# Loading and transposing q and k by units of 192 tokens at the start of a fused attention and feed-forward kernel

## Chip, cores and metric

The kernel runs on one core of a Trainium2 chip. The metric is device time in microseconds (us). The kernel before takes 339.88 us, the median of three runs (338.89 to 340.19). A run over 1.5% above the fastest of its kernel would count as slow. A kernel that ran only once is marked below.

## What is computed

```python
# q, k, v: (8 batches, 8 heads, 576 tokens, 64), fp32
scores = q @ k.T / sqrt(64)                 # per batch and head
mask   = (0 <= i - j) & (i - j < 64)        # sliding window of 64 tokens, causal
attn   = softmax(where(mask, scores, -1e9)) @ v
x      = attn as (4608 tokens, 512)
out    = (relu(x @ w_gate) * (x @ w_val)) @ w_out     # 512 -> 1536 -> 512
```

## The kernel before

A **unit** is 192 tokens of all 8 heads; a batch of 576 tokens is three units. A **tile** of the feed-forward part is two units (384 tokens), so twelve tiles follow each other on TensorE (PE), and the attention of later units is woven between their matmuls. Each instruction stands in its engine's queue in the order in which the program issues it (after the change, GpSimd's trace has the next weights at 24.95 us, behind the cast that the program puts before them and that starts at 24.49). The parts that matter here:

```python
U, UB, G = 192, 3, 4          # tokens of a unit, units of a batch, heads of one half
# S = 576, D = 64; row p = (h, i) of 128 holds 18 tokens of one head: token = 18 i + j

def qk_load(b, name, hh):                       # fp32 -> fp16 cast in GpSimd's DMA
    tile_ = nat[b, name, hh] = a_in.tile([128, S // 32 * D], FP16, ...)
    src = (q if name == "q" else k)[b, G * hh:G * hh + G]
    nc.gpsimd.dma_start(tile_, src.rearrange("h (i j) d -> (h i) (j d)", i=32))

def k_first(hh):                                # k of batch 0: fp32, SyncE's hardware queue
    k32 = nat["k32", hh] = x_sb.tile([128, S // 32 * D], FP32, ...)
    nc.sync.dma_start(k32, k[0, G * hh:G * hh + G].rearrange("h (i j) d -> (h i) (j d)", i=32))
# k_round: ScalarE casts k32 to fp16.  qk_trans: VectorE transposes 128x576 into kT or qT.
# ... cut ...
def w_load(wt, src, f0, f1, landed):            # 512 KB (fp16) of weights, GpSimd's DMA
    ...
    nc.gpsimd.dma_start(dst, part)

# start of the program (cut)
for hh in range(2): k_first(hh)
for hh in range(2): qk_load(0, "q", hh)
heat(12, ...)                                   # dummy matmuls
bands(); constants(); v_ones(1, nc.vector)      # masks on GpSimd, fixed values on VectorE
# then, by planned time: transposes of k and q, v_load(0), v_load(1), the six pieces of
# gate and value weights, v_load(2), three pieces of output weights, q and k of batch 1, ...
```

`v_low` copies 64 rows of the values, so that the 128 rows of a matmul hold the 64 tokens before a window as well. `st` is a score matmul, `pv` the product with the values, `sT` the transposed row sums, `xt` the normalised result that the hidden layer `h` reads, `op` the output matmul.

The softmax here doesn't subtract the row's maximum and nothing guards it: scores larger than these inputs give would overflow.

Of the kernel before, what the change touches and what calls it, by code (L numbers as in the profile page):

```python
# [12 lines left out]
MUL = mybir.AluOpType.mult  # L13

# [28 lines left out]
def kernel(  # L43
# [10 lines left out]
    nc = tc.nc  # L54
# [32 lines left out]
    v16s = [persist.tile([128, UB, H, 128], FP16, name=f"v16_{i}") for i in range(UB)]  # L87
# [27 lines left out]
    def v_ones(i, eng):  # L115
        eng.memset(v16s[i][64 if i == 0 else 0:, 0, :, 64:128], 1.0)
        for w in range(1, UB):
            eng.memset(v16s[i][:, w, :, 64:128], 1.0)  # L118

    def k_zeros():  # L120
        nc.vector.memset(kTs[1][:, :, 0:64], 0.0)

    def constants():
        nc.vector.memset(kTs[0][:, :, 0:64], 0.0)
        nc.vector.memset(v16s[0][0:64, 0], 0.0)
        nc.vector.memset(ones, 1.0)
        nc.vector.memset(ones0, 1.0)
        nc.vector.memset(ones0[0:64], 0.0)

# [40 lines left out]
    def k_first(hh):  # L170

        k32 = nat["k32", hh] = x_sb.tile([128, S // 32 * D], FP32, name="k32", bufs=2)
        nc.sync.dma_start(k32, k[0, G * hh:G * hh + G].rearrange("h (i j) d -> (h i) (j d)", i=32))

    def k_round(hh, part, parts):
        n = S // 32 * D // parts
        if part == 0:
            nat[0, "k", hh] = a_in.tile([128, S // 32 * D], FP16, name=f"k{hh}", bufs=2)
        nc.scalar.copy(nat[0, "k", hh][:, n * part:n * part + n], nat["k32", hh][:, n * part:n * part + n])  # L179
# [8 lines left out]
    def v_load(u):  # L188
        b, uu = divmod(u, UB)
        for w in range(UB):  # L190
            k0 = U * uu + 64 * w
            nc.gpsimd.dma_start(v16s[uu][64:128, w, :, 0:64], v[b, :, k0:k0 + 64].rearrange("h p d -> p h d"))  # L192

    def v_low(u):

        uu = u % UB
        if uu > 0:
            nc.vector.tensor_copy(v16s[uu][0:64, 0, :, 0:64], v16s[uu - 1][64:128, UB - 1, :, 0:64])
        nc.vector.tensor_copy(v16s[uu][0:64, 1:UB, :, 0:64], v16s[uu][64:128, 0:UB - 1, :, 0:64])
# [72 lines left out]
    def u_pv(u, cs=(0, 2, 1, 3)):  # L272
# [3 lines left out]
        v16 = v16s[u % UB]  # L276
# [25 lines left out]
    def u_pv_wide(u):  # L302

        d = units[u]
        v16 = v16s[u % UB].rearrange("p w h d -> p w (h d)")
# [60 lines left out]
    def plan_unit(u, T, exp=0.8, mask=1.5, pv=3.9, copy=(4.7, 6.0), norm=(4.8, 6.1, 7.4, 8.7), gap=0.6):  # L366
# [3 lines left out]
        W.at(T + (3.3 if u == 2 else 1.4 if u < 6 else -2.0), lambda: v_low(u))  # L370
# [14 lines left out]
    def ready(n):  # L385
        while normed[0] < n:
            W.pop()
# [96 lines left out]
    with tc.manual_schedule():  # L484
        for hh in range(2):
            k_first(hh)
        for hh in range(2):
            qk_load(0, "q", hh)
# [6 lines left out]
        heat(12, units[0]["st"][1][3])  # L495
        bands()
        constants()
        v_ones(1, nc.vector)
        for hh in range(2):
            for part in range(2):  # L500
                k_round(hh, part, 2)
        W.at(5.0, lambda: qk_trans(0, "k", 0, 0, 9))
        W.at(5.1, band_bias)
        W.at(5.2, lambda: qk_trans(0, "k", 0, 9, 18))
        W.at(7.0, lambda: qk_trans(0, "q", 0))
        W.at(8.6, lambda: qk_trans(0, "k", 1, 0, 9))
        W.at(8.7, lambda: qk_trans(0, "k", 1, 9, 18))
        W.at(9.9, lambda: qk_trans(0, "q", 1))
        G3, V3, O3 = ([(wt, src, f0, f0 + 4) for f0 in (0, 4, 8)]
                      for wt, src in ((wg, moe_w_gate), (wv, moe_w_val), (wo, moe_w_out)))  # L510
        W.at(5.5, lambda: v_load(0))
        W.at(5.6, lambda: v_load(1))
        W.at(6.4, lambda: w_load(*G3[0], 13.7))
        W.at(6.5, lambda: w_load(*V3[0], 16.3))
        W.at(6.6, lambda: w_load(*G3[1], 18.9))
        W.at(9.9, lambda: w_load(*V3[1], 21.5))
        W.at(9.9, lambda: w_load(*G3[2], 24.1))
        W.at(9.9, lambda: w_load(*V3[2], 26.7))
        W.at(12.3, lambda: v_load(2))
        W.at(12.6, lambda: w_load(*O3[0], 31.2))  # L520
        W.at(12.7, lambda: w_load(*O3[1], 33.8))
        W.at(12.8, lambda: w_load(*O3[2], 36.4))
        plan_batch(1, None, (37.0, 37.8, 39.4, 40.8))
        W.at(13.0, lambda: qk_load(1, "k", 0))
        W.at(13.0, lambda: qk_load(1, "k", 1))
        W.at(13.0, lambda: qk_load(1, "q", 0))
        W.at(13.0, lambda: qk_load(1, "q", 1))
        W.at(13.1, lambda: v_load(3))
        W.at(30.0, lambda: v_load(4))
        W.at(30.1, lambda: v_load(5))  # L530
        W.at(5.3, lambda: u_bias(0))
        W.at(5.4, lambda: heat(11, units[0]["spare"], False))
        W.at(8.7, lambda: u_st(0, (0,)))
        W.at(9.5, lambda: heat(11, units[0]["spare"], False))
        W.at(11.0, lambda: u_st(0, (1,)))
        for g in range(G):
            W.at(9.6 + 0.05 * g, lambda g=g: u_exp(0, g, 0))
            W.at(11.1 + 0.05 * g, lambda g=g: u_exp(0, g, 1))
            W.at(12.0 + 0.05 * g, lambda g=g: u_copy(0, g))
            W.at(12.3 + 0.05 * g, lambda g=g: u_exp(1, g))  # L540
        W.at(11.4, lambda: u_pv(0, (0, 1)))
        W.at(11.35, lambda: u_bias(1, (2, 3)))
        W.at(11.5, lambda: u_pv(0, (2, 3)))
        W.at(11.6, lambda: u_bias(1, (0, 1)))
        W.at(11.7, lambda: u_st(1))
        W.at(11.9, lambda: u_sum(0, 0))
        W.at(11.2, lambda: v_low(0))
        W.at(12.15, lambda: v_low(1))
        W.at(12.1, lambda: u_sum(0, 1))
        W.at(12.2, lambda: u_back(0))  # L550
        W.at(12.5, lambda: u_norm(0))
        W.at(12.6, lambda: u_pv(1))
        W.at(12.7, lambda: u_sum(1, 0))
        W.at(12.8, lambda: u_sum(1, 1))
        for n in range(4):
            W.at(12.9, lambda n=n: u_copy(1, n))
        W.at(13.2, lambda: u_back(1))
        W.at(13.3, lambda: u_norm(1))
        W.at(21.0, lambda: v_ones(2, nc.vector))
        W.at(21.0, lambda: v_ones(0, nc.vector))  # L560
        W.at(22.0, k_zeros)
        fast = 0.8, 1.5, 3.9, (4.1, 5.3), (4.2, 5.4, 6.4, 7.5), 0.5
        plan_unit(2, 23.0, 0.8, 1.5, 3.9, (4.7, 6.0), (4.8, 7.4, 11.2, 11.3), 0.6)
        plan_unit(3, 42.15, *fast)
        plan_unit(4, 49.3)
        plan_unit(5, 56.95, *fast)
        T = 67.0
        early, late = (-7.4, -6.0, -4.6, -3.2), (-20.3, -18.9, -17.5, -16.1)
        for t in range(3, NU // 2):
            for u, at, tr in ((2 * t, T + 0.5, early), (2 * t + 1, T + 13.2, late)):  # L570
                if u == 2 * UB:
                    plan_batch(2, 36.9, (49.3, T + 0.3, T + 1.7, T + 3.1))
                elif u % UB == 0:
                    plan_batch(u // UB, at + tr[0] - 10, [at + x for x in tr])
# [3 lines left out]
        W.advance(13.7)  # L578
        ready(1)
        hidden(0, 0, U, 0, 4, 4)  # L580
        ready(2)
# [44 lines left out]
```

## Time and profile before

| | us |
|---|---|
| first score matmul | 8.81 |
| first hidden matmul (tile 0 starts) | 17.00 |
| tile 0 / tile 1 / tile 2 end | 44.06 / 74.77 / 101.86 |
| each later tile | about 25.95 |
| span of the profiled run | 337.9 |

The times in this table and its counterparts are starts and ends of groups of matmuls, read from the trace. From tile 3 on TensorE has no gaps worth naming (busy for 25.95 of 25.95 us in tile 3), so whatever a change is worth must show in the first four rows. The prediction shows the table of busy time by stretch, the chain of waits and TensorE's waits of this kernel. One line also belongs here. It is from the list of DMA issues on the page of the kernel before (destination and source, issuing queue, count, KB each, median us from issue to landing):

```profile
k<-in_k_dram SPq DMA_DIRECT2D x2, 576.0 KB, 4.0
```

Two fp32 loads of 0.59 MB on SyncE's hardware queue landed 4.0 us after their issue (the median of the two), at about 4.4 and 5.8 us. In the microseconds from 3 to 4 and from 4 to 5, 396 and 406 GB/s moved, all of it in packets of SyncE's queue; those of GpSimd's queue start after 5 us.

### The profile page before, as it was taken

The page shows a single profiled execution, that of the slowest core. Times are in us where ns is not written, and L with a number is a line of the kernel's source. Part 1 is how long each engine was busy: PE and PEld are TensorE (multiplying, and loading weights), DVE is VectorE, ACT ScalarE, POOL GpSimd, SP SyncE. Part 2 cuts the span into 40 slices and gives each one's busy share as a digit, 9 for nine tenths or more (in the row PEclk, how much of TensorE's full clock was granted, in tenths as well). Part 3 has the DMA queues.
Part 4 walks back from the last instruction along what each step waited for, and adds up shares of the span by engine and source line. Part 5 has one row for each costly group of instructions (what it writes and reads, how often), then busy time and mean ns, then how long its engine had stood idle before and what let it go on. Part 6 is the DMA issues. An engine that isn't in the chain of part 4 may idle for free.

```text
span 337.9 us, 8605 instructions
## 1 busy us (share of the span) xinstructions
PE 325.5 (96%) x3522; PEld 197.3 (58%) x3522; DVE 260.3 (77%) x493; ACT 176.7 (52%) x383; POOL 74.0 (22%) x121
## 2 busy tenths in 40 slices
PE   8699998999999999999999999999999999999995
PEld 4485485856546656655655655654655664664653
DVE  5878878998998874897989974888889874884430
ACT  4546165745636646645555564564564664653321
POOL 8724341250213221320210410150120200000000
PEclk9989999999999999999999999999999999999999
DMA  8999998496343933491242853296214402001002
GB/s 214 178 206 193 204 203 135 31 139 98 24 77 49 158 51 71 29 185 70 17 53 73 111 75 98 18 143 123 17 10 111 32 3 93 2 2 71 24 0 94
DMA packets 52886, 29.44 MB, mean 87 GB/s; under 512 B 39280, under 2 KB 44272, under 8 KB 52848
## 3 DMA queue, kind: packets, MB, share of 16 engines
q0 software_dynamic: 47088, 18.29, 47.4%
q1 hardware_dynamic: 5616, 10.55, 8.7%
q8 instruction: 27, 0.44, 0.6%
q14 instruction: 11, 0.09, 0.1%
q10 hardware_dynamic: 144, 0.07, 0.1%
HBM read 37.75 MB, written 9.44 MB: 140 GB/s over the span
## 4 chain that ended last, share of the span: by engine, by line
PE 81%; DVE 13%; issue 3%; DMA 2%; ACT 0%; DVEq 0%; ACTq 0%; POOLq 0%
PE h L419 52%; PE op L433 21%; PE pv L311 5%; PE st L249 3%; DVE sT L341 2%; DVE qT L186 2%; DMA q<-in_q_dram 2%; DVE g_sb L407 2%; DVE kT L186 1%; DVE xt L356 1%; DVE rs L350 1%; DVE p L270 1%; PE op L465 1%; DVE v L118 1%; DVE rT L348 0%
## 5 line engine op out<-in xcount | busy, mean ns | idle before, releaser
L419 PE MATMUL h<-xt,wg 128*128 128x384 f16 (+1 forms) x640 | 117.5, 313 | 1.7 <-DVE xt L356 1.7
L419 PE MATMUL h<-xt,wv 128*128 128x384 f16 (+1 forms) x640 | 116.7, 311 | 1.0 <-DVE g_sb L407 1.0
L407 DVE TENSOR_TENSOR g_sb<-r_sb,h 128x384 f16<-128x384 f32 x144 | 78.3, 550 | 48.8 <-PE h L419 47.1
L404 ACT ACTIVATE r_sb<-h 128x384 f32<-128x384 f32 x144 | 70.2, 492 | 67.0 <-PE h L419 55.3
L433 PE MATMUL op<-wo,g_sb 128*128 128x512 f16 x420 | 93.0, 379 | 0.0
L192 POOL DMA_DIRECT2D v<-in_v_dram x72 | 49.5, 696 | 181.0 <-PE pv L311 95.3
L419 PEld LDWEIGHTS <-wg 128*128 128x128 f16 x640 | 61.5, 99 | 36.5 <-DVE xt L356 1.6
L419 PEld LDWEIGHTS <-wv 128*128 128x128 f16 x640 | 59.0, 98 | 31.7 <-issue 1.3
L433 PEld LDWEIGHTS <-g_sb 128*128 128x128 f16 x420 | 40.3, 98 | 46.6
L341 DVE STREAM_TRANSPOSE sT<-pv 64x384 f32<-64x384 f32 x88 | 51.1, 580 | 9.7 <-PE pv L311 7.7
L329 ACT COPY xv<-pv 64x384 f32<-64x384 f32 x88 | 41.6, 473 | 21.5 <-DVE sT L341 8.1
L440 ACT COPY o_sb<-op 128x512 f32<-128x512 f32 x35 | 20.5, 586 | 54.6 <-PE op L433 54.6
L263 ACT ACTIVATE p<-st 128x384 f16<-128x384 f32 x92 | 39.7, 492 | 4.2 <-PE st L249 4.1
L270 DVE TENSOR_TENSOR p<-p,mask 128x384 f16<-128x384 f16 x88 | 27.5, 352 | 0.3 <-ACT p L263 0.2
L350 DVE STREAM_TRANSPOSE rs<-rT 128x768 f32<-128x768 f32 x24 | 23.5, 978 | 0.8
L356 DVE TENSOR_TENSOR xt<-xv,rs 128x768 f16<-128x768 f32 x24 | 22.8, 948 | 0.8
L311 PEld LDWEIGHTS <-v 128*128 128x128 f16 x528 | 18.6, 98 | 4.2 <-issue 0.8
L186 DVE STREAM_TRANSPOSE kT<-k 128x576 f32<-128x576 f32 (+1 forms) x18 | 19.7, 1121 | 1.4 <-ACT k L179 1.3
L311 PE MATMUL pv<-p,v 128*128 128x64 f16 x528 | 19.7, 193 | 1.1 <-DVE p L270 0.6
L186 DVE STREAM_TRANSPOSE qT<-q 128x576 f32<-128x576 f32 x16 | 18.9, 1239 | 1.1 <-DMA q<-in_q_dram 1.1
L249 PEld LDWEIGHTS <-kT 32*128 32x128 f16 x1152 | 11.0, 92 | 10.0 <-issue 9.9
L249 PE MATMUL st<-qT,kT 32*128 32x64 f16 x1152 | 13.9, 189 | 2.3 <-DVE qT L186 2.0
(47 smaller groups left out, 91.8 us busy)
## 6 DMA issues: line engine op xcount, KB each, us to landing
out_dram<-o_sb SPq DMA_DIRECT2D x35, 256.0 KB, 2.0
q<-in_q_dram POOLq DMA_DIRECT2D x16, 288.0 KB, 8.1
v<-in_v_dram POOLq DMA_DIRECT2D x72, 64.0 KB, 3.2
k<-in_k_dram POOLq DMA_DIRECT2D x14, 288.0 KB, 6.1
wg<-in_moe_w_gate_dram POOLq DMA_DIRECT2D x3, 512.0 KB, 10.1
wv<-in_moe_w_val_dram POOLq DMA_DIRECT2D x3, 512.0 KB, 11.9
wo<-in_moe_w_out_dram POOLq DMA_DIRECT2D x3, 512.0 KB, 13.7
k<-in_k_dram SPq DMA_DIRECT2D x2, 576.0 KB, 4.0
```

The source lines that it names most:

```text
L186: nc.vector.transpose(dst.rearrange("p (i j) -> p j i", i=32)[:, j0:j1], src[:, j0:j1])
L192: nc.gpsimd.dma_start(v16s[uu][64:128, w, :, 0:64], v[b, :, k0:k0 + 64].rearrange("h p d -> p h d"))
L249: nc.tensor.matmul(d["st"][hh][g][:, c:c + 64], kT[rows, hh, ks + 64 * w:ks + 64 * w + 128, dh], qT[rows, hh, ks + 64 * w:ks + 64 * w + 64 ...
L263: nc.scalar.activation(d["p"][g].rearrange("p h c -> p (h c)"), d["st"][0][g][:, 0:2 * U], ACT.Exp, scale=scale)
L270: nc.vector.tensor_tensor(p, p, mask[:, None, :].to_broadcast([128, 2 * UB, 64]), MUL)
L311: nc.tensor.matmul(d["pv"][c % 2][:, c // 2, e, 64 * w:64 * w + 64], v16[:, w, 128 * h - 64 * e:128 * h - 64 * e + 128], d["p"][h % G][:, ...
L329: nc.scalar.copy(d["xs"][rows, n::2], d["pv"][n][rows, :, e, 0:U])
L341: nc.vector.transpose(to[64 * e:64 * e + 64, half::2], d["pv"][half][64 - 64 * e:128 - 64 * e, :, e, 0:U])
L404: nc.scalar.activation(part(r_sb), part(h1), ACT.Relu)
L407: nc.vector.tensor_tensor(g_sb[:, f:f + w, c0:c1], part(r_sb), part(h2), MUL)
L419: nc.tensor.matmul(h[:, b * n:b * n + n], wt[:, c, (f + b) * 128:(f + b) * 128 + 128], xt[:, c, c0:c1], start=(c == 0), stop=(c == NC - 1))
L433: nc.tensor.matmul(op, g_sb[:, f, bass.ds(sub * 128, 128)], wo[:, f], start=(f == 0), stop=(f == NF - 1))
```

## The change

The intent: unit 0 needs only its own 192 tokens. So q and k of batches 0 and 1 are loaded, cast and transposed by units; unit 0's loads are spread over the two hardware queues; fewer bytes stand before the weights; the values of a whole batch share one buffer, and the fixed parts of these buffers are set by GpSimd. Its core, with cuts:

```diff
+    J = U // 32
+    def unit_rows(name, u, hh):
+        b, uu = divmod(u, UB)
+        src = (q if name == "q" else k)[b, G * hh:G * hh + G, U * uu:U * uu + U]
+        return src.rearrange("h (i j) d -> h i (j d)", i=32)
+    def unit_load(name, u, hh):                    # units 2 to 5
+        nc.gpsimd.dma_start(unit_tile(name, u, hh), unit_rows(name, u, hh))
+    def unit_load32(name, u, hh, queue):           # units 0 and 1
+        t32 = nat[name, u, hh, 32] = a_in.tile([128, J * D], FP32, ...)
+        queue.dma_start(t32, unit_rows(name, u, hh))
 ...
+        for name in "kq":
+            unit_load32(name, 0, 0, nc.sync)
+            unit_load32(name, 0, 1, nc.scalar)
         for hh in range(2):
-            k_first(hh)
-        for hh in range(2):
-            qk_load(0, "q", hh)
+            for name in "kq":
+                unit_load32(name, 1, hh, nc.sync)
+        v_load(0)
 ...
-        heat(12, units[0]["st"][1][3])
+        heat(7, units[0]["st"][1][3])
 ...
+        for hh in range(2):
+            for name in "kq":
+                unit_round(name, 1, hh, nc.gpsimd.tensor_copy)
+        w_load(*V3[0], 12.8)
+        v_low(1, nc.gpsimd.tensor_copy)
+        heat(6, units[0]["spare"], False)
+        u_pv(0, (0, 1))
 ...
+        for n in (1, 2):
+            w_load(*G3[n], 15.3 + 5.1 * (n - 1))
+            w_load(*V3[n], 17.9 + 5.1 * (n - 1))
+        v_fixed(0, nc.gpsimd, ((UB, NG), (0, UB)))
+        W.at(12.4, lambda: unit_loads(2))
 ...
-        plan_batch(1, None, (37.0, 37.8, 39.4, 40.8))
+        for u, t in ((2, 25.5), (3, 38.0), (4, 45.0), (5, 52.0)):
+            plan_trans(u, t - 2.4)
+            plan_unit(u, t, *(fast if u < 4 else ()))
```

## The prediction

> **What bounds the kernel now.** I read the table of busy time by stretch first, cut where tiles of 384 tokens end on TensorE (its cuts come from the chain of waits). Columns: stretch and length in us, then busy time (instructions) of PE, PEld, DVE, ACT and POOL, granted clock, DMA share, GB/s.
>
> ```profile
> 17.00:44.06 27.06, 26.56 (x236) 17.34 (x236) 22.84 (x43) 11.58 (x26) 9.63 (x15) 0.94 1.40 197
> 44.06:74.77 30.71, 28.24 (x445) 22.74 (x444) 26.60 (x53) 17.99 (x39) 11.45 (x19) 1.00 0.90 125
> 74.77:101.86 27.09, 26.58 (x279) 15.24 (x277) 24.51 (x43) 14.34 (x31) 3.41 (x5) 1.00 0.49 70
> 101.86:127.81 25.95, 25.95 (x278) 15.04 (x277) 20.50 (x41) 14.46 (x31) 6.97 (x11) 1.00 0.60 93
> ```
>
> From tile 3 on TensorE is busy all of each 25.95 us, and the change leaves that steady part alone. What can be won lies before 101.86: 17.00 us before the first hidden-layer matmul, and three tiles that are longer than their matmuls. Their work, from this trace: 48 full-width matmuls take 7.80 us (0.1625 each), 36 output matmuls 7.77, one attention unit 0.48 for its scores and 0.70 for its values. Tile 0, with one unit beside it, needs 15.6 + 7.77 + 1.18 = 24.55; tile 1, with three units and half-width matmuls (16 in 1.32, so 15.84), needs 15.84 + 7.77 + 3.54 = 27.15. So tile 0 loses 2.5, tile 1 3.6 and tile 2 (against 25.95) 1.1 us: **about 7 us after the start, and 17 us of start**.
>
> Then the chain that ended last, within the start (start, length, what):
>
> ```profile
> 1.31 6.16 DMA q<-in_q_dram
> 7.49 1.26 DVE qT L186
> 8.75 1.08 DVE kT L186 x2
> 9.83 1.09 DVE qT L186
> 10.97 0.36 PE st L249 x21
> ...
> 14.91 0.99 DVE rs L350
> 15.99 0.97 DVE xt L356
> ```
>
> The reader should see a transfer, then transposes in a row, then the attention of unit 0. The first scores wait for q of all 576 tokens although unit 0 uses 192. Next the waits of TensorE in tile 1, 44 to 75 us (waiter, what it waited for, total us, times, longest):
>
> ```profile
> PE h L419 <- DVE xt L356: 1.2, 1, 1.2
> PE h L419 <- DVE g_sb L407: 0.7, 1, 0.7
> PE st L249 <- DVE sT L341: 0.3, 1, 0.3
> PE pv L311 <- DVE p L270: 0.3, 1, 0.3
> ```
>
> 2.5 us of tile 1's 3.6: VectorE, 87% busy there, is late. Last, slices of 1 us show what follows a thin start:
>
> ```profile
> 14.00:15.00 1.00, 0.19 (x1) 0.21 (x2) 0.93 (x5) 0.96 (x3) 0.82 (x2) 1.00 1.30 222
> 17.00:18.00 1.00, 0.99 (x7) 0.92 (x7) 1.00 (x4) 0.40 (x2) 0.00 (x0) 0.50 1.25 209
> ```
>
> The granted clock falls to 0.50 from 17 to 20 us: the first 32 hidden matmuls took 4.12 us (17.00 to 21.12) instead of 2.64.
>
> [...]the microsecond from 4 to 5 moved 406 GB/s, and 3 to 4 moved 396. [...]clock 0.50 for about 3 us after four microseconds with 0.69, 0.19, 0.66 and 0.47 us busy. [...]the value copy of 64x1024 takes 0.41 to 0.48 us elsewhere, and 0.65 at 31.01, beside a GpSimd DMA issue. That matters for the casts and memsets that go to GpSimd.
>
> **The change part by part.**
>
> *Loads of unit 0.* Before, k (1.18 MB in fp32), q (1.18) and part of the values stood ahead of the first scores. Now it is four pieces of 0.197 MB, 0.79 in all, two on SyncE and two on ScalarE. The first k piece (0.59 MB) took 3.6 us from issue at 0.81 to landing, data flowing from about 1.75. At 400 GB/s, 0.79 MB plus a little of the values take 2.2 us, so all four are in by about 4.3 (estimate). VectorE then casts two (0.35 each, an estimate from its copy rate), transposes four of 128x192 (288 wide took 0.70 and 576 wide 1.24, hence 0.52) and makes the bias (0.17): about 6.5, against 10.93 for the last transpose before. The bias, whose mask GpSimd makes after three value issues (3 x 0.69 from 1.3, then 1.3 of masks), comes at 4.7 to 5.5, so bias matmuls (0.86) and first scores end near 6.7 and second scores near 7.3, against 11.33.
>
> *Unit 0 to xt.* From second scores to the last sum transpose took 3.04 us before (10.97 to 14.01): 10.4 now. **Here the change gives time back:** the four transposes of unit 1 (4 x 0.52 = 2.1) now stand in VectorE's order between these sums and the reciprocal; before, all had been transposed. They need GpSimd's four casts; GpSimd reaches them at 7.6 (values 2.1, gate weights 0.8) and at some 0.5 each (memsets of 64 and 128 elements took 0.19 and 0.24, so 0.14 + 0.32, an estimate) has them by 9.6. Then 12.5; reciprocal, back transpose and product (2.4 as before) give xt at 14.9. TensorE's order also has unit 1's scores (to 13.05), its exponentials (1.65) and values ahead of the hidden layer: 15.3. So **hidden starts at about 15.3 against 17.0**. Unit 1's sums, reciprocal and product take 3.5 after that: 18.9 to 19.2. Its half of the hidden layer started at 21.12, so 1.9 us are won whether or not the clock halves again, since unit 1's xt ends last.
>
> *Weights.* Two weight pieces landed 2.55 us apart before (gate 0 at about 15.3, value 2 at 28.8, seen at the issues that wait for them), 411 GB/s of fp32. Now 2.36 MB stand ahead of them, not 3.15, so about 2 us earlier, perhaps 3. They ran about 3 us ahead of use before, so this only keeps pace with the earlier start: 0 by itself.
>
> *Memsets.* Five of about 0.5 us and one of 0.17 leave VectorE (24.6 to 28.2); GpSimd gets 2.6 us before unit 2's loads and 2.5 before unit 3's. Tile 0 has slack on VectorE; 0.2 won.
>
> *Unit 2 loaded after the weights.* Its k and q (0.79 MB, 2 us) can land only at about 27; its scores stand in TensorE's order behind 32 half-width and 44 full-width matmuls (9.8 us) from 19, near 29, with up to 2.1 us of transposes between. A stall of 0 to 2 us; I book it as nil net with the 0.9 us of tile 0's waits that go.
>
> *Units 3 to 5.* Scores of unit 3 now stand after 4 half-width matmuls of tile 1, before after 32: 28 x 0.0825 = 2.3 us earlier, so the 1.2 us wait for xt goes. VectorE gets eight transposes of 0.52 (4.2) for three of 1.24 (3.7): about even. I take 1.5 of tile 1's 3.6 and 0.5 of tile 2's 1.1.
>
> Sum: 1.9 + 0.2 + 1.5 + 0.5 = **4.1 us**, so 339.9 - 4.1 = 335.8.
>
> **Rivals.** (a) GpSimd becomes the bound: casts of 1 us each, a value copy of 64x1536[...] delay the later weights by 3 to 4 us, and TensorE stalls at unit 2's scores or at the output weights. For: all further weights queue behind these on one in-order engine. Against: some 3 us of weight slack. Time: 337.5 to 339. (b) VectorE stays the bound in tile 1, its sum of work unchanged, and only the start is won: 337.5. For: 87% busy and the same three units. Against: it idled 4.1 us there. (c) All goes well: unit 0 ready at 14, clock kept, tiles 1 and 2 at nearly their matmuls: 17.0 - 14.0 + 1 + 3 + 0.8, so about 332. Unlikely, since unit 1's transposes sit in the path.
>
> **Range and chances.** (a) and (b) bound one side, (c) the other: 332.8 to 338.4. Faster by over 2% needs under 333.1, close to (c): 0.10. Slower by over 2% would need a new stall of over 10 us: 0.01.
>
> **What would show it.** First hidden matmul at 15.3 (14.3 to 16); xt of unit 1 near 19; unit 1's transposes and GpSimd's casts on the chain of waits, no longer the DMA of q; TensorE waiting under 1 us at unit 2's scores; tile 1 near 29.2 and later tiles at 25.95. Casts over 0.7 us, or waits for weights, would speak for (a); tile 1 still over 30 for (b).

## The result

The changed kernel takes 358.67 us, the median of four runs (355.97 to 361.26), against 339.50 of the kernel before in the same rounds (338.89 to 340.19). The ratio is 1.056, with a 95% interval of 1.048 to 1.065. Ratios in this document are the mean time of one kernel's fast runs over that of the other's of the same rounds, so not quite the ratio of the medians. **The change makes the kernel 5.6% slower; the prediction, 335.8 us, was wrong.**

| us | before | after | added |
|---|---|---|---|
| first score matmul | 8.81 | 15.81 | |
| first hidden matmul | 17.00 | 28.72 | 11.7 |
| tile 0 | 27.06 | 30.22 | 3.2 |
| tile 1 | 30.71 | 32.86 | 2.2 |
| tile 2 | 27.09 | 26.70 | -0.4 |
| span | 337.9 | 354.3 | 16.4 |

The profiled run of the changed kernel is the fastest of its four, with a mean granted clock of 0.995 (the share of full speed that the profile records for TensorE). The other three took 1.7 to 5.3 us longer, at 0.967 to 0.986. So the table explains 16.4 of the 19.2 us between the medians.

The table of busy time by stretch of the changed kernel, cut at its own tiles (stretch, length, busy us (instructions) of PE, PEld, DVE, ACT and POOL, granted clock, DMA share, GB/s):

```profile
28.72:58.94 30.22, 26.17 (x239) 17.00 (x238) 19.19 (x38) 11.55 (x26) 20.00 (x26) 0.97 1.41 172
58.94:91.80 32.86, 29.38 (x447) 23.42 (x446) 29.97 (x60) 17.73 (x39) 23.18 (x37) 1.00 1.50 175
91.80:118.50 26.70, 26.26 (x277) 15.08 (x276) 23.41 (x41) 14.31 (x31) 7.44 (x12) 1.00 0.72 101
118.50:144.45 25.95, 25.95 (x278) 15.01 (x276) 20.52 (x39) 14.63 (x31) 6.95 (x11) 1.00 0.60 93
```

Tile 3 takes 25.95 us as before, so nothing changed in the steady part. The loss is in the start and in tiles 0 and 1. In tile 1 VectorE (DVE) is busy for 29.97 us, where it had been 26.60.

The start first. Single microseconds of it, in the same columns; from the kernel before, while its k loads run:

```profile
4.00:5.00 1.00, 1.00 (x4) 0.30 (x2) 0.00 (x0) 0.60 (x2) 1.00 (x3) 1.00 1.02 406
```

and from the kernel after, while its unit loads run:

```profile
14.00:15.00 1.00, 0.56 (x4) 0.53 (x4) 1.00 (x4) 0.00 (x0) 0.00 (x0) 1.00 0.32 78
20.00:21.00 1.00, 1.00 (x18) 0.55 (x17) 0.00 (x0) 0.00 (x0) 0.00 (x0) 1.00 0.31 75
```

The last two columns carry the verdict: 406 GB/s have become 75 to 78, and the DMA share sits at 0.31 to 0.32 of 16 engines, some five engines' time. (It adds up the times of packets and goes over 1 where they overlap, as in the 1.41 and 1.50 of the table above.) The data is not slow because much else is moving; eleven engines' time is not used (16 less five, an estimate from that share). (PE's busy 1.00 at 20 us is mostly dummy matmuls.) Below, VectorE's own order of time in the kernel after (start, us, engine, line, operation, out<-in, and in brackets the idle time before it and what ended it):

```profile
9.68 0.36 DVE L196 CAST ku<-k 128x384 f16<-128x384 f32 x1 [7.34 <-DMA k<-in_k_dram]
...
13.45 0.36 DVE L196 CAST qu<-q 128x384 f16<-128x384 f32 x1 [2.85 <-DMA q<-in_q_dram]
13.84 0.52 DVE L204 STREAM_TRANSPOSE qT<-qu 128x192 f32<-128x192 f32 x1
14.21 0.17 DVE L115 TENSOR_SCALAR bias<-mask 128x64 f16<-128x64 f16 x1
```

VectorE sits idle for 7.34 and 2.85 us until pieces of k and q land. The bias stands behind them in its order, and TensorE's first scores behind the bias. TensorE's and GpSimd's waits up to 28.7 and 45 us (waiter, what it waited for, us in total, times, longest):

```profile
PE st L233 <- DVE bias L115: 10.0, 1, 10.0
```

```profile
POOL ku L196 <- DMA k<-in_k_dram: 10.7, 2, 8.4
POOL qu L196 <- DMA q<-in_q_dram: 4.6, 2, 2.3
```

Last, the chain of waits of the kernel after, up to 32 us (start, length, what):

```profile
5.89 15.76 DMA k<-in_k_dram
...
21.71 0.51 POOL ku L196
...
24.95 0.76 POOL wv L153
```

A load of 0.197 MB, issued behind others of its kind, takes 15.76 us from issue to landing. GpSimd (POOL) then casts, and only after its last cast issues the next weights, at 24.95 us.

**Why the loads are slow.** The landings (semaphore events in the trace) say more than the rate. For a load of k in the kernel before, the trace has 16 steps, all between 3.96 and 4.37 us. For each of the eight unit loads on the hardware queues, only four come with the data (for the first: 6.39, 6.69, 6.83 and 6.99 us); the only other one comes before any data (2.17 us). The packets of the trace agree. In the kernel before, those of SyncE's two k loads fill 16.3 engines' time from 3 to 4 us and from 4 to 5. In the changed kernel, those of SyncE's and ScalarE's queues together fill 3.8 to 4.3 in each microsecond from 4 to 12, and those of SyncE's alone 3.6 from 14 to 15 and from 20 to 21. So the unit loads run on about four engines of 16, on two queues as on one. That is an estimate from these steps and packet times, since the trace names no engine; "four engines" below means this.

What differs is the access pattern of the source. That of a whole batch folds (head, i) into one dimension of 128 rows, and the load has 16 steps with its data. The source of a unit has 192 of 576 tokens of each head, so head and i no longer fold: its dimensions are 4 heads, 32 rows, 384 elements, and **4 is the slowest**. Whether the four steps come from this dimension is what the first three runs below test (16 steps at 32 rows in e1_heads, four at 4 heads in e2_before4, half the DMA share at 2 heads in e1_pairs). The landings come at 6.99, 9.66, 12.77 and 13.42 us (unit 0) and 16.15, 18.93, 21.65 and 24.44 us (unit 1). From 13.42 on they are 2.72 to 2.79 us apart, 0.197 MB each: some 71 GB/s.

Transfers that others issued come late too, in four of their 16 steps. The first value load (64 KB, GpSimd's queue) reached twelve of its 16 steps by 5.77 us and the last four only at 10.96 to 11.98; the first gate weights twelve by 12.48 and the last four at 26.60 to 27.16. Four is as many as a unit load has with its data, so the estimate is that these steps wait on the same four engines.

**The start lost time in a second place.** From the end of unit 0's second scores to the first hidden matmul it took 5.68 us before and takes 10.57 after. TensorE's own order of time, before:

```profile
10.97 0.36 PE L249 MATMUL st<-qT,kT 32*128 32x64 f16 x24 [0.49 <-DVE qT L186]
...
11.69 0.28 PE L289 MATMUL pv<-p,v 128*64 128x64 f16 x6
```

and after:

```profile
17.64 0.51 PE L273 MATMUL st<-qT,kT 32*128 32x64 f16 x24
19.23 1.44 PE L240 MATMUL st<-zero 128*128 128x256 f16 x6 [1.08 <-ACT p L289]
20.60 0.37 PE L313 MATMUL pv<-p,v 128*64 128x64 f16 x6
```

The change put six dummy matmuls (`st<-zero`) between the scores and the value products. They wait 1.08 us for exponentials and take 1.44, so the products start 2.45 us after the scores and not 0.36. Unit 1's transposes stand for 1.4 us before the reciprocal, and TensorE runs at about half its rate: the dummy matmuls of 128x256 start every 0.20 us, not every 0.11 as before. It had just stood idle for 10.0 us. (The granted clock of this trace reads 1.00 there; e1_heads has the same 0.20 us at a granted clock of 0.50, so the record of this run seems to miss the slow stretch.) VectorE does not wait for unit 1's data here: it starts these transposes at 24.28 us, right behind the last sum transpose. So of the 11.7 us of later start, 6.8 had passed by the end of the second scores, for late data of unit 0, and 4.9 came after it, from the new order and the slow TensorE together.

In tile 0 TensorE waits for unit 2, whose k and q were issued behind the weights, 11.4 us before they landed, and for a weight (its waits from 28.7 to 58.94 us):

```profile
PE h L443 <- DVE g_sb L431: 2.7, 1, 2.7
PE h L443 <- DMA wv<-in_moe_w_val_dram: 0.9, 1, 0.9
```

The 2.7 us are a product `g_sb` that stands on VectorE behind a transpose waiting 3.6 us for that k. In tile 1 (58.94 to 91.8 us):

```profile
PE st L273 <- DVE sT L365: 1.8, 2, 1.2
PE st L273 <- DVE qT L204: 0.7, 2, 0.5
PE pv L335 <- DVE p L294: 0.7, 2, 0.4
```

The wait for `xt` that the prediction wanted gone has gone, but waits for VectorE come to 3.2 us in all, where they were 2.5. That is not all of the 2.2 us that tile 1 lost: TensorE's busy time grew too, from 28.24 to 29.38 us, which no run explains.

### The profile page after: what moved, and what is told of

Read it like the earlier page. It is cut to its first block, busy times and chain, and to the rows that moved or that the text cites. A ratio compares the mean times of both kernels' runs of the same rounds, so it can differ in the third digit from the quotient of the medians.

```text
span 354.3 us, 8620 instructions
## 1 busy us (share of the span) xinstructions
PE 327.7 (93%) x3523; PEld 198.5 (56%) x3523; DVE 257.1 (73%) x483; ACT 176.4 (50%) x381; POOL 90.4 (26%) x141
## 4 chain that ended last, share of the span: by engine, by line
PE 75%; DVE 9%; DMA 8%; issue 3%; POOL 2%; SPq 1%; ACT 1%; DVEq 0%; ACTq 0%; POOLq 0%
PE h L443 47%; PE op L457 20%; PE pv L335 4%; DMA k<-in_k_dram 4%; DMA ku<-in_k_dram 3%; PE st L273 3%; DVE sT L365 3%; SPq L193 1%; DVE qT L211 1%; DVE xt L380 1%; DVE g_sb L431 1%; DVE kT L211 1%; PE op L489 1%; DVE qT L204 1%; POOL wv L153 1%
## 5 line engine op out<-in xcount | busy, mean ns | idle before, releaser
L443 PEld LDWEIGHTS <-wg 128*128 128x128 f16 x640 | 60.7, 99 | 36.6 <-issue 3.1
L273 PE MATMUL st<-qT,kT 32*128 32x64 f16 x1152 | 15.1, 192 | 5.1 <-DVE qT L204 2.0
L273 PEld LDWEIGHTS <-kT 32*128 32x128 f16 x1152 | 11.8, 94 | 13.1 <-issue 11.8
L211 DVE STREAM_TRANSPOSE kT<-k 128x576 f32<-128x576 f32 x12 | 14.7, 1238 | 0.2
L211 DVE STREAM_TRANSPOSE qT<-q 128x576 f32<-128x576 f32 x12 | 14.1, 1238 | 0.0
```

Of the source, the lines that this page charges most:

```text
L211: nc.vector.transpose(dst.rearrange("p (i j) -> p j i", i=32)[:, j0:j1], src[:, j0:j1])
L273: nc.tensor.matmul(d["st"][hh][g][:, c:c + 64], kT[rows, hh, ks + 64 * w:ks + 64 * w + 128, dh], qT[rows, hh, ks + 64 * w:ks + 64 * w + 64 ...
L443: nc.tensor.matmul(h[:, b * n:b * n + n], wt[:, c, (f + b) * 128:(f + b) * 128 + 128], xt[:, c, c0:c1], start=(c == 0), stop=(c == NC - 1))
```

## The experiments

The theory after the result: **(T1)** the shape of the unit loads confines them to four engines, where other transfers wait for them, and that is most of the loss; **(T2)** GpSimd's casts, which stand before the weights in its order (at 24.49 and 24.95 us), hold these back; **(T3)** the rest is VectorE in tile 1. The rivals: the second hardware queue, GpSimd's work or the change of order alone would do it, and the load shape merely rides along. T1 turns out to be half right: the confinement is shown (four steps with the data and 3.6 engines' time, against 16 and 16.3), but the new order takes its own share of the start. All times below are against runs of the kernel before on the same chip (medians 338.8 to 339.4 us). Where only one run was made, the text says so. A table at the end has all of them.

### Each unit load cut by head: e1_heads

```diff
-        queue.dma_start(t32, unit_rows(name, u, hh))
+        rows = unit_rows(name, u, hh)
+        for g in range(G):
+            queue.dma_start(t32[32 * g:32 * g + 32], rows[g])
```

The slowest dimension is now 32 rows, at the price of four times the DMAs. In the expectations from here to e5_free, Theory A is T1, and Theory B is a rival that explains the loss without the slowest dimension.

> The changed kernel with each fp32 load of units 0 and 1 cut by head: four DMAs of 32 rows of 1536 B on the same queue for one of 4 x 32 rows. Same bytes, same rows, same queues, nothing else changed. Theory A[...]: unit 0 all landed by about 6 us, unit 1 by about 12, first hidden matmul at 15 to 17 us instead of 28.7, gate 0 landed by 12 to 14, total 336 to 342 us. Theory B (short rows of 1536 B, or three queues at once, are what is slow): the loads keep some 75 GB/s and the total stays at 353 or more.

It took 352.87 us (351.92 to 353.75), ratio 1.040 with an interval of 1.037 to 1.043. That is far from Theory A's 336 to 342 and next to Theory B's 353; the landings decide. All 16 steps of a load now come one by one (2.33 to 2.66 us for the first), and unit 0 has landed by 9.32 us instead of 13.42, unit 1 by 20.12 instead of 24.44. Scores start at 11.47 us and the hidden layer at 24.10, 4.6 us earlier than after the change, and still 7.1 us later than before it. One limit is now issue, and it is the program's own: eight semaphores take turns on these queues, and from the ninth on each load waits for the semaphore of the load eight before it. SyncE waits 5.2 us in all for that, in eight waits, so unit 1's casts on GpSimd run from 15.55 to 20.76 us and the next weights leave at 20.72. The table by stretch of this kernel shows what that does:

```profile
20.00:21.00 1.00, 0.14 (x19) 0.23 (x22) 1.00 (x3) 0.00 (x0) 0.74 (x2) 1.00 0.00 0
```

DMA share 0.00: no transfer at all, since the next weights have only just been issued. This supports T1, with 5.8 of the 19 us won back, and T2.

### The load shape alone, in the kernel before: e2_before4

```diff
-        nc.sync.dma_start(k32, k[0, G * hh:G * hh + G].rearrange("h (i j) d -> (h i) (j d)", i=32))
+        nc.sync.dma_start(k32, k[0, hh:H:2].rearrange("h (i j) d -> h i (j d)", i=32))
```

Every second head, so that the four heads no longer fold into one dimension; nothing else changes. The heads of k are mixed up (the result still within tolerance; why was not looked into).

> The kernel before with its two k loads of batch 0 reading every second head, so that the source keeps a slowest dimension of 4 heads and does not fold to 128 rows. Same bytes, same rows of 4608 B, same queue; batch 0 of the result is wrong on purpose. Theory A: the two loads of 0.59 MB go at 70 to 110 GB/s, k of half 0 lands at 7 to 10 us instead of 4.4 and half 1 at 13 to 18 instead of 5.8, q behind them late too, total 346 to 354 us. Theory B (row length or the number of queues): nothing changes, 338 to 342 us.

It took 359.23 us (one run), 19.8 more than the kernel before. The chain of waits of this kernel has one line for it:

```profile
1.58 25.07 DMA k<-in_k_dram
```

The same 0.59 MB on the same queue, 4.0 us in the kernel before, now take 25 us: the two halves of k land at 16.64 and 26.65 us instead of 4.4 and 5.8, four steps of each with the data, and the hidden layer starts at 36.49. **The access pattern of the source is the whole difference here**, with no unit loads, no casts on GpSimd and no new order. So the shape alone confines a load to four steps and delays the start. The delay is larger than expected (7 to 10 and 13 to 18 us, 346 to 354 in all): the two loads moved at some 48 GB/s, beside q and the values on GpSimd's queue (69 GB/s at a DMA share of 0.28 from 14 to 15 us).

### Two heads in each DMA: e1_pairs

The same edit as e1_heads with two heads in each DMA, so the slowest dimension is 2.

> The changed kernel with each fp32 unit load cut in two DMAs of two heads (slowest dimension 2). Theory A: two engines instead of four, so about half the rate of after (36 GB/s instead of 72): the eight loads end at about 45 us instead of 24.5, first hidden matmul near 50, total 375 to 395 us. Theory B: more and smaller DMAs of the same rows change little, 352 to 362 us.

It took 373.6 us (one run), just under Theory A's 375 to 395. A microsecond of its start:

```profile
20.00:21.00 1.00, 0.00 (x0) 0.00 (x0) 0.00 (x0) 0.00 (x0) 0.00 (x0) 1.00 0.14 41
```

About half the DMA share (0.14, against 0.31 after the change) and half the rate (41 GB/s, against 75): with more and smaller DMAs the kernel took 373.6 us where the slowest dimension shrank with them, and 352.87 us (e1_heads) where it did not. So here it is that dimension and not the number or size of DMAs.

### Units 0 and 1 on GpSimd's queue: e3_swdge

```diff
-        for name in "kq":
-            unit_load32(name, 0, 0, nc.sync)
-            unit_load32(name, 0, 1, nc.scalar)
-        for hh in range(2):
-            for name in "kq":
-                unit_load32(name, 1, hh, nc.sync)
-        v_load(0)
+        unit_loads(0)
...
+        v_load(0)
+        unit_loads(1)
```

GpSimd's DMAs cast to fp16 on the way, so the casts go as well.

> The changed kernel with units 0 and 1 loaded as units 2 to 5 are, by casting DMAs from GpSimd, and no casts on the engines; same source shape of 4 x 32 rows. Theory A as seen at unit 2 of after (16 landings, 0.79 MB in some 3.3 us): the software queue is not held to four engines, so unit 0 lands by about 7 us, unit 1 by about 11, first hidden matmul at 15 to 18 us, total 336 to 344 us. If the shape of the source limits the software queue too, the loads stay at 75 GB/s and the total stays at 353 or more.

It took 347.63 us (347.44 to 348.32), ratio 1.025 (1.022 to 1.028). Scores start at 9.27 us and the hidden layer at 22.20. The landings of these loads are also four with data and twelve early, but not in the same order each time. The first load has twelve steps at once (3.30 to 3.46 us) and four with its data (5.74 to 6.54). The second has eight at once, four right behind the first load's (5.99 to 6.73) and four at 7.08 to 7.29; the third has only four at once, and fours at 6.21 to 6.94, 7.33 to 7.47 and 7.86 to 8.02. Each of these loads thus has one more group of four steps that comes late. That each occupies four engines more is the estimate from these landings; the trace names no engine.

Unit 0 has landed by 8.64 us and unit 1 by 13.95, somewhat later than the expected 7 and 11. With that, 11.0 of the 19 us are won back, by the loads and the casts together. What binds the start now is the new order, with TensorE at half its rate as after the change (dummy matmuls every 0.20 us): the second scores end at 11.61 us, only 0.3 us later than in the kernel before, and yet 10.59 us pass from there to the first hidden matmul, as after the change (10.57; before 5.68). Unit 1's data lies ready while VectorE reaches its transposes only at 17.75 us. GpSimd issues the first weights late, at 12.46 us behind 14 DMAs of about 0.7 us, but TensorE waits for no weight in the start or in tile 0. So the rival "change of order" is right for some 5 us, of which no run separates the order from the slow TensorE.

### One hardware queue instead of two: e4_onequeue

```diff
-            unit_load32(name, 0, 1, nc.scalar)
+            unit_load32(name, 0, 1, nc.sync)
```

> The changed kernel with all four loads of unit 0 on SyncE's queue, none on ScalarE's. If both hardware queues use the same four engines, the second queue gave nothing: unit 0 all landed near 13.4 us as in after (two queues), unit 1 near 24.5, total 354 to 362 us. If ScalarE's queue had its own engines, unit 0 now lands 2 to 5 us later and the total grows by as much over after's 356 to 361.

It took 358.31 us (one run), within the range of the changed kernel. Unit 0's last piece lands at 14.52 us instead of 13.42, unit 1's at 27.38 instead of 24.44. If the two queues used different engines, one queue alone would have taken about twice as long for unit 0 (an estimate), and the packets of both together fill only 3.8 to 4.3 engines' time after the change. So the second queue gives unit 0 1.1 us. What it gives in all is not shown: first scores start at 14.46 us, 1.4 earlier than with two queues, but unit 1 lands 2.9 us later and the hidden layer starts that much later, and the one total lies within the noise.

### The weights freed of the casts: e5_free

```diff
-        for hh in range(2):
-            for name in "kq":
-                unit_round(name, 1, hh, nc.gpsimd.tensor_copy)
         w_load(*V3[0], 12.8)
+        for n in (1, 2):
+            w_load(*G3[n], ...); w_load(*V3[n], ...)
 ...
+                unit_round(name, 1, hh, nc.scalar.copy)
```

The loads keep their four engines; unit 1 is cast by ScalarE, and the weights are issued right behind the first piece.

> The changed kernel, loads still 4 x 32 rows, but unit 1's casts go from GpSimd to ScalarE and the five later weight loads are issued right behind the first; the value copy of unit 1 stays on GpSimd, behind them. If the casts that hold GpSimd's queue are the main cause (rival a of the prediction): hidden layer 4 us or more earlier and the total falls below 350. If the four engines are (theory A), the weights now compete on those four with unit 1, which lands later than 24.5 us, and the total is no better than after: 354 to 366 us.

It took 354.78 us (one run), 3.9 less than the median of the changed kernel but only 1.2 less than its fastest. From 20 to 21 us 229 GB/s move instead of 75 (DMA share 1.26 instead of 0.31): weights now move beside the unit loads. But the hidden layer starts even later, at 29.88 us. Unit 0's last piece lands at 14.56 us instead of 13.42, beside the weights, and the first scores start as much later; from there on nothing changes (10.60 us from the second scores to the hidden layer), though unit 1 lands at 25.8. The weights were not quite freed either: GpSimd issues the second piece at 7.72 us and the next four at 12.92 to 22.13, each after a wait for the semaphore of a value load whose last four steps come late. What was won is the wait inside tile 0. What was expected if the casts were the main cause (hidden layer 4 us earlier, under 350 in all) did not come.

### Both: e6_both

The edits of e1_heads and e5_free together.

> Both remedies: loads of units 0 and 1 by head (16 engines) and weights not held by GpSimd's casts. Theory: the two causes add. Unit 0 lands by 9.5 us as in e1_heads, unit 1 by 16 to 20 beside the weights, no idle stretch of the DMA engines between 14 and 22 us, hidden layer from 19 to 22 us, no wait for weights; total 343 to 349 us (e1_heads 352.9). Rival (the casts do not matter once unit 1 is in time): 351 to 354.

It took 350.12 us (349.51 to 350.71), ratio 1.031 (1.028 to 1.035), between the two expectations and not the sum of the two gains: the hidden layer starts at 26.20 us, later than e1_heads, because unit 1's late DMAs now move beside the weights (unit 1 landed at about 22 us, in e1_heads at 20.12). But tile 0 has no gap over 0.25 us, and the whole is 2.8 us shorter than e1_heads, which is what T2 is worth there. So with both hindrances eased, but in the new order, loading by units still starts 9 us later than loading the batch.

### Batch 0 whole again, the rest of the change kept: e7_batch0

Here `k_first`, `k_round`, `qk_load` and `qk_trans` of the kernel before load and transpose batch 0, with its dummy matmuls. The weights right behind the values, the values by batch, GpSimd's memsets and units 3 to 5 by units stay.

> Batch 0 loaded and transposed whole, as in the kernel before (128 rows of 4608 B), with the weights right behind the values; from unit 2 on the changed kernel: units 3 to 5 by unit, values by batch, memsets on GpSimd, its times. It shows what the rest of the change is worth. Theory (my prediction's second half: tile 1 gains 1.5, tile 2 0.5, memsets 0.2): hidden layer from 16.5 to 17.5 us, total 336 to 339 us. Rival (the later unit loads cost as well, through waits for their transposes): tile 1 is 31 us or longer, total 340 to 345.

It took 342.54 us (341.81 to 342.68), ratio 1.009 (1.005 to 1.013). **Some 16 of the 19 us have gone with the start by units**: its loads, casts, late weights, dummy matmuls and order together, which this run does not tell apart. What is left is 3 us, as the rival expected: the start at 17.96 instead of 17.00, and tile 1, whose line is

```profile
45.50:78.30 32.80, 29.31 (x446) 23.28 (x444) 29.27 (x57) 17.73 (x39) 19.94 (x31) 1.00 1.56 170
```

32.80 us, as in the changed kernel (32.86), with the same three waits of TensorE (1.8, 0.7 and 0.7 us). Tile 1's loss does not come from the late start. The 0.96 us of the start are in VectorE's order and GpSimd's order of time:

```profile
14.05 1.52 DVE L234 COPY v<-v 64x1536 f16<-64x1536 f16 x1
```

```profile
13.04 2.12 POOL L121 MEMSET v<- 128x1536 f32 x2
```

The value copy takes 1.52 us while GpSimd sets memory, and ends 0.41 us after it (14.05 + 1.52 = 15.57, against 13.04 + 2.12 = 15.16).

### Transposes of units 3 to 5 earlier: e8_early

```diff
-                plan_trans(u, t - 2.4)
+                plan_trans(u, t - 5.4)
```

> e7_batch0 (batch 0 whole, batch 1 by units) with the transposes of units 3 to 5 placed 3 us earlier in VectorE's order. Theory A (TensorE waits for scores' sums in tile 1 because VectorE reaches these transposes too late, not because it has more to do): the two waits of st (1.8 and 0.7 us) shrink to under 1 us together, tile 1 31.3 to 31.8 instead of 32.80, in all 341 to 341.7. Theory B (VectorE's sum of work in tile 1, 29.27 us against 26.6 in the kernel before, is what counts): tile 1 stays at 32.4 or more, in all 342 to 343.

It took 341.56 us (340.62 to 343.32), ratio 1.009 (1.005 to 1.012): not told apart from e7_batch0 in time. From the first hidden matmul to the end of tile 1 it took 59.97 us against 60.34. Tile 1 itself takes 33.45 us, longer than Theory A's 31.3 to 31.8, though the total falls in its range. TensorE waits in other places, hardly less. So the place of these transposes in VectorE's order is not the main cause.

### Batch 1 whole as well: e9_batch1

```diff
+        plan_batch(1, None, (32.9, 33.7, 35.3, 36.7))
+        for name in "kq":
+            for hh in range(2):
+                W.at(13.1, lambda name=name, hh=hh: qk_load(1, name, hh))
...
-            W.at(13.1 + 0.1 * u, lambda u=u: unit_loads(u))
```

> e7_batch0 with batch 1 loaded and transposed whole as well (four calls of 576 tokens instead of twelve of 192 for units 2 to 5), the rest of the change kept. If the per-unit transposes are what lengthens tile 1: VectorE's work there falls by about 1.5 us, tile 1 30.3 to 31.2 instead of 32.80, in all 340 to 341. If it is the other parts (values by batch, new order of units 2 to 5): tile 1 stays over 32, in all 342 to 343.

It took 340.67 us (339.88 to 341.58), ratio 1.005 (1.002 to 1.008). Tile 1 takes 31.60 us, with VectorE busy for 27.82 instead of 29.27: transposes by units cost VectorE 1.45 us there, and TensorE 1.2. The expected 30.3 to 31.2 were missed by 0.4, so something else is left.

### GpSimd's memset moved: e10_memset

```diff
-        v_fixed(0, nc.gpsimd, ((UB, NG), (0, UB)))
+        W.at(12.9, lambda: v_fixed(0, nc.gpsimd, ((UB, NG), (0, UB))))
```

This is e9_batch1 with that memset issued behind the last weights. The first case of the expectation is that the memset beside the copy makes it slow.

> e9_batch1 with GpSimd's memset of the value buffer of batch 0 issued behind the last weight load instead of beside the value copy of unit 1. [...](64x1536 copy 1.52 us instead of about 0.55): copy at 0.5 to 0.6, first hidden matmul at 17.0 instead of 17.96, in all 0.8 to 1.1 us below e9_batch1. If the copy is slow for another reason: copy still at 1.5, no difference (under 0.3 us).

It took 341.45 us (338.63 to 342.35), ratio 1.006 (1.002 to 1.011). The two value copies of the start (count: least, median and greatest ns, then first and last start) in e9_batch1

```profile
L234 DVE COPY v<-v x2: 422/954/1486, 10.9 to 14.1; 64x1024 f16<-64x1024 f16 x1, 64x1536 f16<-64x1536 f16 x1
```

and in e10_memset

```profile
L234 DVE COPY v<-v x2: 512/534/555, 10.8 to 14.0; 64x1024 f16<-64x1024 f16 x1, 64x1536 f16<-64x1536 f16 x1
```

The larger copy, beside which GpSimd set memory from 13.04 to 15.14 us in e9_batch1, falls from 1.49 to 0.56 us, and the hidden layer starts at 16.88 instead of 17.94. The memset beside it was the cause, as expected; **the total did not move**. Tile 0 now ends at 42.70 us, 1.4 before that of the kernel before, and then TensorE waits 1.9 us for q of batch 1. 5 us of memsets stand on GpSimd ahead of its loads; the next run asks whether that is why. The wait that was taken away at the start (1.06 us) came back where this transfer landed.

### Memsets behind the loads: e11_order (wrong result)

```diff
-        W.at(12.9, lambda: v_fixed(0, nc.gpsimd, ((UB, NG), (0, UB))))
+        W.at(12.9, lambda: v_ones(0, 2 * UB, NG))
+        W.at(14.0, lambda: v_ones(0, 0, 2 * UB))
...
-        W.at(13.0, lambda: v_fixed(1, nc.gpsimd))
+        W.at(13.2, lambda: v_fixed(1, nc.gpsimd))
```

> e10_memset reached the end of tile 0 at 42.70 us (44.06 in the kernel before) and then waited 1.9 us for q of batch 1, whose loads stood on GpSimd behind 5 us of memsets. Here only the memset that unit 2 needs (128x768) stays ahead of those four loads; the others go behind them. If the memsets delay the loads: q of batch 1 transposed by about 43 instead of 45.2, tile 0 still ends at 42.7 to 43, tile 1 takes 31 to 32 instead of 34.60, in all 336.5 to 338.5, under the kernel before by 0.1 to 0.7%. If the loads wait for bandwidth behind the output weights anyway (they queue behind 2.4 MB of them): q still at 45, in all 340 to 341.5.

The result was wrong (relative error 0.59), by a mistake in the edit: the late memset writes ones over rows of the first group that must stay zero. Its time stands for what it is: 339.06 us (338.76 to 340.87), ratio 1.000 (0.998 to 1.002). q of batch 1 was transposed by 44.9 us, neither the expected 43 nor much before the 45.2 of e10_memset. So the memsets were not what held q back: without them GpSimd waits for earlier weights to land instead, and issues q at 29.75 to 31.1 us where it had been 30.4 to 31.5. In its order of time on VectorE and on GpSimd,

```profile
44.96 1.99 DVE L237 COPY v<-v 64x1024 f16<-64x1024 f16 x1
```

```profile
45.27 1.41 POOL L125 MEMSET v<- 128x1536 f32 x1
```

the moved memset fell beside the next value copy, which took 1.99 us instead of about 0.5.

### Memsets in GpSimd's gaps: e12_slots

The same memsets with the zeros kept, each put where GpSimd only waits to issue the next weights or k of batch 1.

> e11_order mended (the zeros stay) and all memsets of the value buffers put into gaps in which GpSimd only waits to issue the output weights and batch 1's k (gaps of 1.1 to 2.4 us between 18 and 29 us). If the memsets were what was left: first hidden matmul 16.9, value copy of 64x1024 back at 0.4 to 0.6 instead of 1.99, tile 0 ends near 43, tile 1 takes 30.3 to 31.3, in all 336.7 to 338.3 (0.2 to 0.7% under the kernel before). If tile 1 is bound by VectorE's work or the loads whatever the memsets do: tile 1 over 31.8, in all 339 or more.

The result is right, and the time 339.29 us (339.05 to 341.23), ratio 1.002 (1.000 to 1.004): above the expected 336.7 to 338.3. Tiles 0 and 1 and TensorE's longest waits from 16.8 to 76 us:

```profile
16.89:42.70 25.81, 25.17 (x239) 16.19 (x239) 18.63 (x34) 11.35 (x26) 14.27 (x19) 1.00 1.33 201
42.70:75.10 32.40, 29.12 (x445) 23.06 (x443) 28.54 (x52) 17.76 (x39) 18.54 (x29) 1.00 1.51 165
```

```profile
PE h L457 <- DVE xt L394: 1.7, 2, 1.1
PE pv L349 <- DVE p L308: 1.1, 2, 0.7
PE st L287 <- DVE qT L225: 1.1, 1, 1.1
```

Tile 0 is 1.25 us shorter than in the kernel before, and tile 1 is 1.69 longer: in part the 1.1 us wait for q of batch 1 (`qT`), whose second half VectorE could only transpose at 43.52 us, when it had landed. The memsets are not what was left. What else holds tile 1 was not taken apart.

### All runs

The time of tiles 0 and 1 is counted from the first hidden matmul to the end of tile 1. No run beats the kernel before.

| | time, us | ratio | hidden starts | tiles 0 and 1 |
|---|---|---|---|---|
| before | 339.50 | | 17.00 | 57.77 |
| after | 358.67 | 1.056 | 28.72 | 63.08 |
| e1_heads | 352.87 | 1.040 | 24.10 | 65.4 |
| e1_pairs | 373.6 (1 run) | | 47.49 | 61.9 |
| e2_before4 | 359.23 (1 run) | | 36.49 | 57.9 |
| e3_swdge | 347.63 | 1.025 | 22.20 | 61.0 |
| e4_onequeue | 358.31 (1 run) | | 31.62 | 62.5 |
| e5_free | 354.78 (1 run) | | 29.88 | 60.7 |
| e6_both | 350.12 | 1.031 | 26.20 | 60.0 |
| e7_batch0 | 342.54 | 1.009 | 17.96 | 60.34 |
| e8_early | 341.56 | 1.009 | 17.83 | 59.97 |
| e9_batch1 | 340.67 | 1.005 | 17.94 | 59.26 |
| e10_memset | 341.45 | 1.006 | 16.88 | 60.42 |
| e11_order (wrong result) | 339.06 | 1.000 | 16.85 | 58.45 |
| e12_slots | 339.29 | 1.002 | 16.89 | 58.21 |

No run has the unit loads with all 16 steps and the old order of the dummy matmuls and transposes together. Whether any form of unit load would start earlier than the whole batch is open.

## Why the prediction was wrong

**Loads of unit 0: the step that failed.** "At 400 GB/s, 0.79 MB plus a little of the values take 2.2 us, so all four are in by about 4.3 (estimate)." They were in at 13.42. The bytes were right, and the rate was carried over from loads of another shape: some 71 GB/s is what the unit loads gave, with four steps each, and e2_before4 shows that the shape alone does it (some 48 GB/s there). A second queue adds little here: unit 0 had landed by 13.42 us with two and by 14.52 with one (e4_onequeue). No view of the kernel before held a load of this shape, and the diff shows the shape.

**Unit 0 to xt: the second step that failed.** Expected 15.3 for the first hidden matmul, measured 28.72. Unit 0's data, 9.1 us later than assumed, is only part of it. From the second scores (7.3) to the hidden layer the prediction has 8.0 us; it took 10.57, and 10.59 in e3_swdge, where unit 1's data was in time. The durations behind it were right: casts of 0.36 us on VectorE and 0.51 on GpSimd (0.35 and 0.5 expected), transposes of 0.52, which overlap, so that four take 1.4 us and not 2.1. What the sum left out are the dummy matmuls ahead of the value products, 2.1 us, and TensorE at half its rate after standing idle (10.0 us here, 3.4 in e3_swdge), of which the prediction's own reading of the clock (0.50 for about 3 us, behind four thin microseconds) had warned. Even with the loads as fast as predicted the hidden layer would have started near 17.9 (7.3 + 10.6, an estimate from these two runs), no earlier than the 17.0 before. (A slip besides: the 3.04 us run from the start of the second scores, and were added to their end.)

**Weights.** "0 by itself" failed with it: the later weights left GpSimd at 24.95 to 29.3 us (the last of them at 12.6 in the kernel before), behind casts that wait for loads. (The prediction's two ends, 15.3 and 28.8, are five steps of 2.7 us, not 2.55.) This is rival (a), in a form that it did not have: not the time of the casts (0.51 us each), but the waits ahead of them in GpSimd's order (10.7 us for k and 4.6 for q). Work of VectorE and GpSimd at the same time cost something as well: the copy of 64x1536 beside a memset took 1.5 us and not 0.56, worth 1 us of start (e10_memset). The trace that the prediction gave for this (0.65 against 0.41 to 0.48 us) was too weak to size it.

**Unit 2 loaded after the weights.** A stall of 0 to 2 us was booked as nil; TensorE waited 2.7 us for a product behind unit 2's k. It came later than the estimate for the reason of the weights.

**Units 3 to 5.** "About even" on VectorE, and 1.5 us won in tile 1: measured 32.86 us instead of 30.71, VectorE 29.97 busy instead of 26.60. e9_batch1 puts 1.2 us of that on transposes by units. The wait for `xt` was removed, as predicted, and replaced by waits for `sT`, `qT` and `p`. This is rival (b), which expected tile 1 to stay as it was; it became longer. Tile 2 won 0.4 of the 0.5 expected.

**The chances.** "Slower by over 2% would need a new stall of over 10 us: 0.01." Such a stall came: 10.0 us for the bias. The chance was set from stalls that the view of the kernel before could show, and no view of that kernel had a DMA of the new shape in it. The memsets were misread by one: six of about 0.5 us left VectorE, not five; nothing hung on it.

The intent itself, fewer bytes ahead of unit 0, was never tested at the rate that it assumed: no form of unit load tried here had it.

## What to carry to other kernels

When a load is cut into smaller ones, write down the access pattern of its source and look at the slowest dimension before reusing a measured rate: 0.79 MB in loads with four steps arrived by 13.42 us here, three times as many bytes in loads with all 16 by 9.39. When instructions are put in a new order, count everything that now stands between two steps of the longest chain, dummy work included. Don't put work that waits for a late transfer on the engine that also issues the next transfers (GpSimd waited 15.3 us for k and q here, and the next weights left at 24.95 us), and don't put memsets on GpSimd beside VectorE's copies (1.5 us instead of 0.56 here). After a start has been shortened, look at once for the next transfer that the faster kernel will wait for; here what was won before 43 us (1.4 us in e10_memset) was lost in tile 1 again.

## What the runs measured of loads, copies and issue

- By the microsecond, with little else moving, loads with a slowest dimension of 4 gave 69 to 79 GB/s (95 once) and those of 2 gave 34 to 45, where loads of 128 rows gave 406. Over four, two and 16 engines that is 17 to 25 GB/s for each (an estimate from these rates).
- Beside such loads, DMAs with 16 steps had four late ones: a 64 KB value load reached twelve steps at 5.77 us and its last four at 10.96 to 11.98; the first 512 KB weight piece took 20.2 us from issue to landing instead of 6.9.
- Four DMAs of 32 rows each, with 16 steps each (e1_heads, 352.87 us), beat one of 4 x 32 rows with four (358.67).
- VectorE's copy beside a memset on GpSimd: 64x1536 took 1.49 to 1.65 us instead of 0.56, and 64x1024 took 1.99 instead of 0.42 to 0.58, although the trace has it start 0.31 us before the memset (times on GpSimd are rough).
- In the changed kernel SyncE's last three unit loads, with no semaphore to wait for, occupied it for 2.56, 3.83 and 2.43 us, the first three for 0.71 to 0.90.
